# Delta-rule recurrence with a feed-forward: the first three chunks and the last taken unit by unit

## The chip, the cores and the metric

The kernel runs on one core of a Trainium2 chip. The metric is the device time of one execution in microseconds. The core has five engines with queues of their own: TensorE (PE; its weight loads are listed apart as PEld), VectorE (DVE), ScalarE (ACT), GpSimd (POOL) and SyncE (SP, which issues most DMAs).

## The reference

Two stages, one behind the other. The first is a gated delta rule over 768 time steps for 4 batches and 8 heads of width 48; the second is a feed-forward of width 2048 with a tanh GELU on the 3072 tokens of 384 values that come out of the first.

```python
k_n = k / (np.linalg.norm(k, axis=-1, keepdims=True) + 1e-06)
state = np.zeros((B, H, D, D))
for t in range(S):
    y[:, :, t] = np.einsum('bhd,bhde->bhe', q[:, :, t], state)
    v_old = np.einsum('bhde,bhd->bhe', state, kt)
    state = state + bt[..., None, None] * np.einsum('bhd,bhe->bhde', kt, vt - v_old)
x = y.transpose(0, 2, 1, 3).reshape(B * S, H * D)
h = x @ w_in
g = 0.5 * h * (1.0 + np.tanh(c * (h + 0.044715 * h * h * h)))
return g @ w_out
```

## The kernel before, in words

Time is cut into 12 chunks of C = 64 steps. The partition axis holds two batches of 64 steps each, so a chunk has two units of 128 rows, unit u = 2c + x with x = 0, 1; the units of one chunk belong to different batches and share no state.

`prep(u)` makes what a unit needs and what does not depend on the state: it normalises k (`kn`), multiplies by beta (`kb`), casts q (`qb`), transposes all three (`T` on PE and the copy `kT` for the first six units, a transposing DMA on SP behind them), takes two products of the transposed tiles (`G2` and `G`, L624 and L616), masks them into `ln` and `wp` (DVE), and inverts a triangular 64 x 64 matrix for each head by five rounds. A round is a product on PE (`A`, L665), a subtraction from 2I on DVE (`rt` or `rl`, L679), a second product (`B`, L665) and a copy out of PSUM into the block-diagonal tile `bd` or the result `xi` (L448 on ACT or DVE, L647 and L651 on POOL).

`chain(c)` is the recurrence over chunks, for both units at once: state times k (`K`, L720), minus v (`R`, L730, on DVE), state times q (`Q`, L720), inverse times that (`U`, L742), its copy `us` (`Un`), the new state (`S`, L751, and `Sn`), the output (`O`, L765), its copy `xo` (`On`), and the transposition of the output into `xT` (`X`, L787 and a copy, or a transposing DMA for chunks 4 to 10). `U`, `K`, `Q`, `S` and `O` are 32 matmuls each on small tiles of the PE array (64 x 64 or 48 x 64); the products of the inverse and the feed-forward use the full 128 x 128 array.

`mlp(gi)` is the feed-forward of one chunk, 256 tokens: 48 up matmuls (`up`, L809, 128 columns of W1 against 256 tokens, in groups of three), a GELU on ACT for every 4 of the 16 slices (`gelu`, L814, 128 x 1024), 2 x 16 down matmuls (`down`, L822, 384 columns, in groups of four), a copy `ob` (`Z`) and two output DMAs for each 128 tokens. W1 and W2 are loaded by POOL's DMA queue (L546, L550).

The order of the work on each engine is fixed when the program is built. Class `Flow` collects the steps with a duration, a key and the tiles read and written; `schedule()` is a planner that plays the engines forward in time and takes the ready step of the lowest key, with rules for PSUM banks, for PE's changes between full and small tiles (`SWITCH`, `PEN`, `GLUE`), for its clock and for blocks of 256 instructions (`BLOCK`, `REFILL`). `KEYS` shifts the key of every kind of step and `EXTRA` that of one kind in one part (`F.part`, the chunk) of the kernel. 110 matmuls on a tile of zeros (`fill`, L505) have the highest key and are placed where PE has nothing else ready; those left over stand at the end of PE's queue. `emit()` writes each engine's queue out with semaphore waits; an engine never leaves its queue's order at run time.

Of the kernel before, what the change touches and what calls it, by code (L numbers as in the profile page):

```python
# [14 lines left out]
C = 64  # L15
# [9 lines left out]
class Flow:  # L25
# [5 lines left out]
    SLACK = 0.128241  # L31
# [3 lines left out]
    STALL_SLACK = 0.120045  # L35
    YIELD = 0.372832
    KEYS = {"A": (-12.24992, -5.03297), "B": (-9.6185, -29.0564), "G": (-8.95358, -2.60127), "G2": (-14.50399, -54.31342),
# [3 lines left out]
            "Z": (-21.81342, -68.60243), "bdc": (7.59004, 13.93148), "bde": (-0.21638, -43.1126), "bdz": (1.14496, 67.13998),  # L41
            "down": (12.66804, 33.19835), "eps": (30.23541, -44.34922), "gelu": (6.25889, 47.5543), "inv": (-36.99569, -17.04963),
            "kT": (21.81306, -1.95089), "kb": (-10.85643, 26.05958), "kn": (46.26391, 23.16738), "ladj": (-19.15066, 56.95864),
            "ln": (21.15613, -25.11016), "loadk": (6.01406, -22.83934), "loadq": (13.08921, -8.18376), "loadv": (3.59665, -5.26042),
            "out": (5.42829, -58.1066), "pow": (4.89602, -34.99663), "qb": (7.55526, 19.94565), "rt": (-22.59389, 3.94263),
            "sq": (-11.42456, 52.70149), "sum": (35.6419, -19.11125), "tabG": (-30.0791, 50.43816), "tri": (19.11756, -10.52721),
            "turn": (-4.97863, -20.83721), "turnx": (-24.1172, -42.56893), "up": (4.18149, -12.91155), "w1": (-25.34548, 32.61637),
            "w2": (31.31702, 12.2471), "wp": (0.57459, -43.94026), "xT": (-28.12189, -41.44086), "xi": (5.37624, -27.34308)}
    EXTRA = {"1eps.1": 5.8983, "1inv.1": -0.10911, "1pow.1": -12.59508, "1sq.1": 17.11214, "1sum.1": -2.50147, "1wz.0": -1.64746,
# [324 lines left out]
def bass_deltanet__then__act_gelu_tanh_kernel(  # L374
# [15 lines left out]
    GROUPS = [[c] for c in range(NC)]  # L390
# [9 lines left out]
    with nc.allow_non_contiguous_dma("strided loads"), nc.allow_low_precision("bf16 pipeline"):  # L400
# [173 lines left out]
        def prep(u):  # L574
            x, c = u % 2, u // 2
            z = "" if c else "0"
# [118 lines left out]
        def chain(c):  # L695
            ss = [(2 * c + x) % NP for x in range(2)]
            z = "" if c else "0"
# [3 lines left out]
            so, sn, son, snn = st[c % 2], st[(c + 1) % 2], f"st{c % 2}", f"st{(c + 1) % 2}"  # L701
            rb, rbn, ub, ubn, xb, xbn = rs[c % 2], f"rs{c % 2}", us[c % 2], f"us{c % 2}", xo[c % 2], f"xo{c % 2}"
            vr, vrn = raw["v"][c % NR], [f"vraw{c % NR}{x}" for x in range(2)]
            key = 2 * c + 0.5
            each = [(x, g) for x in range(2) for g in range(4)]

            def flat(ap):
                return ap.rearrange("p y x g d -> p y (x g d)")

            def banks(ap):  # L710
                return ap.rearrange("p (y r) -> p y r", y=2)[:, :, 0:DM]

            def at(name, P, r, b, x, g):
                o = 512 * b + 4 * D * x + D * g
                return P(ps(name))[r, o:o + D]

            def ks(e, P, y, name):
                for x, g in each:
                    for p, a in quad:
                        ins = e.matmul(at(name, P, hf(a), p, x, g), kT[ss[x]][hf(p, D), y, g, hf(a)], so[hf(p, D), a, x, g, :],  # L720
                                       start=(x == 0 and g == 0), stop=(y == 0), skip_group_check=True)
                return ins
            if first:
                for x in range(2):
                    A("act", z + "R0", lambda e, P, x=x: e.activation(
                        rb[:, :, x, :, :], vr[:, H * x:H * x + H, :].rearrange("p (g y) d -> p y g d", y=2), ACT.Copy, scale=-1.0), 0.5,
                      reads=[vrn[x]], writes=[rbn + "ab"[x]], key=key)
            else:
                A("pe", z + "K", lambda e, P: ks(e, P, 0, "K"), 0.28, reads=n("kT") + [son], alloc=(ps("K"), 2), mode="t", key=key, mm=32)
                A("dve", z + "R", lambda e, P: e.tensor_tensor(  # L730
                    rb[:, :, :, :, :].rearrange("p y x g d -> p y (x g) d"), banks(P(ps("K"))).rearrange("p y (g d) -> p y g d", d=D),
                    vr[:, :, :].rearrange("p (g y) d -> p y g d", y=2), ALU.subtract), 0.98,
                  reads=vrn, frees=[ps("K")], writes=[rbn + "a", rbn + "b"], key=key)
                A("pe", z + "Q", lambda e, P: ks(e, P, 2, "O"), 0.28, reads=n("kT") + n("xi") + [son, rbn + "a", rbn + "b"], alloc=(ps("O"), 2), mode="t",
                  key=key + 0.1, mm=32)
# [113 lines left out]
        for u in range(NU):  # L849
# [7 lines left out]
            if u % 2:  # L857
                chain(u // 2)
# [33 lines left out]
```

## Time and profile before

| | |
|---|---|
| timed runs | 278.71, 283.88, 285.86 us; median 283.88 |
| profiled execution | 278.1 us, of which the span from first to last instruction is 276.1 |
| mean granted TensorE clock | 0.994 |
| busy PE, DVE, ACT, POOL | 264.4, 193.8, 173.4, 142.5 us |
| first up matmul (L809), last down matmul (L822) ends | 46.33, 271.40 us |

The page's costliest groups are given as line, engine, operation, out<-in and the number, then busy time and mean length of one in ns, then the idle time of the engine just before them and what ended it. The slices cut the span into 40 equal parts; a digit is the busy share in tenths. Matmuls are pipelined, so the length of one is longer than its share of PE's time; the distance between the starts of two neighbouring groups is what a group costs.

```profile
L809 PE MATMUL ps<-xT,W 128*128 128x256 bf16 x576 | 81.7, 273 | 0.1
L822 PE MATMUL ps<-W,gT 128*128 128x384 bf16 x384 | 74.4, 326 | 0.1
L448 ACT ACTIVATE bd<-ps 64x512 bf16<-64x512 f32 x92 | 53.3, 589 | 20.2 <-PE ps L665 18.8
L814 ACT ACTIVATE gT<-ps 128x1024 bf16<-128x1024 f32 x48 | 48.6, 1023 | 18.2 <-PE ps L809 18.1
L679 DVE TENSOR_TENSOR rt<-ps,two 128x512 bf16<-128x512 f32 x72 | 48.6, 685 | 15.4 <-PE ps L665 15.0
```

### The profile page before, as it was taken

Reading aid. Unit: us, or ns where it says so; the run is one execution under the profiler, and the core shown is the slowest. Engines: PE = TensorE matmul, PEld = TensorE weight load, DVE = VectorE, ACT = ScalarE, POOL = GpSimd, SP = SyncE. Lnnn points to the kernel's source line nnn. Section 1 sums busy time; section 2 is a strip of 40 time slices with the busy share of each in tenths; the row PEclk is TensorE's granted clock in tenths of the full one; section 3 lists DMA queues with packets and bytes.
Section 4 is the critical chain, followed back from the end, with each engine's and each line's share of the span. In section 5 each row is a group of like instructions: output and inputs, shape, how many; then the busy total and the mean of one; then the engine's idle time right before and its main releaser. Section 6 shows DMA issues by size and latency. Waiting matters only on the chain.

```text
span 276.1 us, 12595 instructions
## 1 busy us (share of the span) xinstructions
PE 264.4 (96%) x5684; PEld 199.6 (72%) x5696; DVE 193.8 (70%) x308; ACT 173.4 (63%) x265; POOL 142.5 (52%) x214
## 2 busy tenths in 40 slices
PE   8999767999999999899999999999999999999999
PEld 3656456877777766786785878788788767996864
DVE  8899985898559989787978789677784638551000
ACT  5845474786847769885674566677777434875530
POOL 3178162689927985997958876245242403220000
PEclk9999997999999999999999999999999999999999
DMA  7999999993996977897299943717520282300213
GB/s 122 168 149 193 188 191 161 151 169 74 195 167 146 179 133 151 156 158 108 58 139 127 168 96 70 135 33 139 96 59 2 62 145 51 43 2 2 57 31 85
DMA packets 116309, 31.49 MB, mean 114 GB/s; under 512 B 110368, under 2 KB 115488, under 8 KB 116256
## 3 DMA queue, kind: packets, MB, share of 16 engines
q1 hardware_dynamic: 111920, 27.24, 60.7%
q0 software_dynamic: 2880, 3.15, 7.0%
q8 instruction: 45, 0.74, 1.2%
q10 hardware_dynamic: 1456, 0.30, 0.6%
q14 instruction: 8, 0.07, 0.1%
HBM read 20.64 MB, written 4.72 MB: 92 GB/s over the span
## 4 chain that ended last, share of the span: by engine, by line
PE 88%; DVE 5%; issue 2%; ACT 2%; DMA 2%
PE ps L822 23%; PE ps L809 22%; PE ps L665 18%; PE ps L505 9%; PE ps L742 3%; PE ps L616 3%; PE ps L720 2%; DMA kT<-tok 2%; PE ps L765 2%; PE ps L624 2%; PE ps L600 2%; DVE rt L679 1%; PE ps L751 1%; DVE wp L633 1%; ACT bd L448 1%
## 5 line engine op out<-in xcount | busy, mean ns | idle before, releaser
L809 PE MATMUL ps<-xT,W 128*128 128x256 bf16 x576 | 81.7, 273 | 0.1
L822 PE MATMUL ps<-W,gT 128*128 128x384 bf16 x384 | 74.4, 326 | 0.1
L448 ACT ACTIVATE bd<-ps 64x512 bf16<-64x512 f32 x92 | 53.3, 589 | 20.2 <-PE ps L665 18.8
L814 ACT ACTIVATE gT<-ps 128x1024 bf16<-128x1024 f32 x48 | 48.6, 1023 | 18.2 <-PE ps L809 18.1
L679 DVE TENSOR_TENSOR rt<-ps,two 128x512 bf16<-128x512 f32 x72 | 48.6, 685 | 15.4 <-PE ps L665 15.0
L809 PEld LDWEIGHTS ps<-xT,W 128*128 128x128 bf16 x576 | 48.9, 98 | 6.0
L647 POOL TENSOR_SCALAR_AFFINE_SELECT bd<-ln 64x512 bf16<-64x512 bf16 x48 | 31.5, 656 | 37.3 <-DVE ln L628 32.7
L822 PEld LDWEIGHTS ps<-W,gT 128*128 128x128 bf16 x384 | 33.8, 98 | 17.4 <-ACT xi L448 0.2
L651 POOL COPY bd<-xi 64x256 f32<-64x256 f32 x64 | 25.4, 398 | 36.7 <-ACT xi L448 27.6
L448 ACT ACTIVATE xi<-ps 128x512 bf16<-128x512 f32 x48 | 28.3, 596 | 13.7 <-PE ps L665 13.2
L633 DVE CAST_PREDICATED wp<-mup,ps 128x1024 bf16<-128x1024 uint16 x24 | 29.0, 1214 | 1.2 <-PE ps L616 1.0
L505 PE MATMUL ps<-wz 128*128 128x512 bf16 x98 | 27.7, 411 | 2.1 <-DVE wz L454 1.3
L448 DVE CAST bd<-ps 64x512 bf16<-64x512 f32 x36 | 24.6, 688 | 6.5 <-PE ps L665 5.9
L665 PE MATMUL ps<-rt,bd 128*128 128x64 bf16 x576 | 28.6, 193 | 0.6 <-DVE rt L679 0.3
L679 DVE TENSOR_TENSOR rl<-ps,two 128x384 bf16<-128x384 f32 (+1 forms) x48 | 23.1, 487 | 8.4 <-PE ps L665 7.9
L665 PE MATMUL ps<-wp,bd 128*128 128x64 bf16 (+1 forms) x576 | 27.6, 188 | 1.4 <-DVE wp L633 0.4
L665 PEld LDWEIGHTS ps<-wp,bd 128*128 128x128 bf16 x576 | 23.2, 97 | 7.0 <-DVE wp L633 1.7
L568 POOL TENSOR_TENSOR nrm<-nrm,half 128x16 f32<-128x16 f32 x9 | 26.1, 2908 | 3.7 <-DVE nrm L565 3.4
L665 PEld LDWEIGHTS ps<-rt,bd 128*128 128x128 bf16 x576 | 23.5, 98 | 4.7 <-DVE rt L679 1.8
L592 POOL TENSOR_TENSOR tok<-tok,bsb 128x384 bf16<-128x384 bf16 x23 | 19.0, 843 | 14.9 <-PE ps L751 8.7
L448 ACT ACTIVATE ob<-ps 128x384 f32<-128x384 f32 x21 | 10.3, 491 | 18.3 <-PE ps L822 18.1
L628 DVE CAST_PREDICATED ln<-mlo,ps 128x512 bf16<-128x512 uint16 x24 | 16.5, 687 | 6.4 <-PE ps L624 6.1
(83 smaller groups left out, 329.3 us busy)
## 6 DMA issues: line engine op xcount, KB each, us to landing
qraw<-in_q_dram SPq DMA_DIRECT2D x24, 192.0 KB, 5.1
vraw<-in_v_dram SPq DMA_DIRECT2D x24, 192.0 KB, 5.0
out_dram<-ob SPq DMA_DIRECT2D x48, 96.0 KB, 2.4
kraw<-in_k_dram SPq DMA_DIRECT2D x22, 192.0 KB, 5.0
W<-in_moe_w_in_dram POOLq DMA_DIRECT2D x2, 768.0 KB, 10.2
W<-in_moe_w_out_dram POOLq DMA_DIRECT2D x2, 768.0 KB, 14.8
kT<-tok SPq DMA_TRANSPOSE x18, 5.1
kraw<-in_k_dram ACTq DMA_DIRECT2D x2, 96.0 KB, 3.1
```

The costliest lines, as they stand in the source:

```text
L448: return e.activation(out, in_, ACT.Copy) if e is nc.scalar else e.tensor_copy(out, in_)
L505: ins = e.matmul(P(name)[:, :], wz[:, 0:128], wz[:, 0:512])
L568: e.tensor_tensor(nr[:, 1, hx], nr[:, 0, hx], half[:, hx], ALU.pow), {"act": 0.22, "pool": 1.65 * wd},
L592: A(POOL, z + "kb", lambda e, P: e.tensor_tensor(kb, kn, bcol, ALU.mult), tt, reads=[n("tok0"), *BS], writes=[n("tok1")], key=u)
L633: A("dve", z + y, lambda e, P, lo=lo, hi=hi: e.copy_predicated(wp[s][:, :, lo:hi], mup[:, lo:hi].bitcast(U16).unsqueeze(1).to_broadcast([1 ...
L647: A("pool", z + "X1", lambda e, P, src=src, dst=dst: e.affine_select(out=dst, in_=src, compare_op=ALU.not_equal, fill=1.0, base=0, pattern ...
L651: A("pool", z + "bdc", lambda e, P, src=src, dst=dst: e.tensor_copy(dst.bitcast(F32), src.bitcast(F32)), 0.42, reads=[n("xi")], writes=[w( ...
L665: ins = e.matmul(P(name)[:, C * h + lo:C * h + C], bd[m][:, h, :], rhs[:, h, lo:C], start=not add, stop=True, skip_group_check=add)
L679: e, r_[:, :, lo:C], P(ps(f"A{i}")).rearrange("p (h t) -> p h t", h=H)[:, :, lo:C]) if u < ADD else e.tensor_tensor(
L809: ins = e.matmul(P(ph)[:, w * f:w * f + w].rearrange("p (x t) -> p x t", x=2), W1[:, j, 128 * (i + f):128 * (i + f) + 128], x_[:, :, j, :] ...
L814: A("act", z + "gelu", lambda e, P, i=i, ph=ph: e.activation(g_[:, i:i + nf, 0:w], P(ph).rearrange("p (f t) -> p f t", f=nf), ACT.Gelu_app ...
L822: ins = e.matmul(P(po)[:, 0:DM], g_[:, f, 128 * b:128 * b + 128], W2[:, f, :], start=(f == 0), stop=(f == FC - 1))
```

## The change

`chain` and `mlp` take a list `xs` of the units of the chunk that they work on. For the first three chunks (`HALVES`) and the last (`TAIL`) they are called for one unit at a time, as soon as that unit is prepared; the other eight chunks are called for both units, as before. A call for one unit issues 16 small-tile matmuls in place of 32 for each step of the recurrence, copies of half the width, three transposes in place of six, and 48 up matmuls of 128 columns for 128 tokens, with a GELU of 128 x 1024 for every 8 slices. The tiles `st`, `rs`, `us`, `xo`, `xT` and `gT` are tracked by unit and not by chunk. The number of GELUs, down matmuls, loads and outputs stays. `F.part` is the unit in place of the chunk, so `EXTRA` has an entry by kind and unit, and all the planner's constants, `KEYS` and `EXTRA` have new values; so the order of the work on every engine is another throughout.

```diff
-    SLACK = 0.128241
+    SLACK = 1.796034
...
-    STALL_SLACK = 0.120045
-    YIELD = 0.372832
...
+    STALL_SLACK = 7.031178
+    YIELD = 0.145092
...
-    PEN = 3.376955
-    HOLD = 0.200936
-    SOON = 0.200469
-    GLUE = 4.720138
-    PATIENCE = 0.264186
-    HASTE = 0.586658
+    PEN = 3.089705
+    HOLD = 0.543568
+    SOON = 0.261360
+    GLUE = 3.285667
+    PATIENCE = 0.831901
+    HASTE = 8.000000
...
-    PHASE = 1.896137
+    PHASE = 0.429894
...
-    GROUPS = [[c] for c in range(NC)]
+    HALVES, TAIL = 3, 1
...
-        def chain(c):
+        def chain(c, xs):
             ss = [(2 * c + x) % NP for x in range(2)]
-            z = "" if c else "0"
-            n = lambda y: [f"{y}{s}" for s in ss]
-            ps = lambda y: f"{y}.{c}"
+            x0, nx = xs[0], len(xs)
+            sl = slice(x0, x0 + nx)
+            z = "" if 2 * c + x0 else "0"
+            n = lambda y: [f"{y}{ss[x]}" for x in xs]
+            m = lambda y, i: [f"{y}{i}{x}" for x in xs]
+            ps = lambda y: f"{y}.{c}.{x0}"
...
-            key = 2 * c + 0.5
-            each = [(x, g) for x in range(2) for g in range(4)]
+            key = 2 * c + (0.5 if nx == 2 else x0)
+            tt = 0.16 + 0.00107 * 384 * nx
+            each = [(x, g) for x in xs for g in range(4)]
...
-            A("pe", z + "U", umat, 0.36, reads=n("xi") + [rbn + "a", rbn + "b"], alloc=(ps("U"), 2), mode="t", key=key, mm=32)
...
+            A("pe", z + "U", umat, 0.18 * nx, reads=n("xi") + rbn, alloc=(ps("U"), nx), mode="t", key=key, mm=16 * nx)
...
-        def mlp(gi):
-            g = GROUPS[gi]
+        def mlp(c, xs):
             z = ""
-            w = 256 * len(g)
...
+            x0, nx = xs[0], len(xs)
+            sl, w = slice(x0, x0 + nx), 128 * nx
+            ts = slice(128 * x0, 128 * x0 + w)
...
             nf = 1024 // w
...
         for u in range(NU):
-            F.part = u // 2
+            F.part = u
...
             prep(u)
-            if u % 2:
-                chain(u // 2)
-            for gi, g in enumerate(GROUPS):
-                if u == 2 * g[-1] + 1:
-                    mlp(gi)
+            c = u // 2
+            for xs in ((u % 2,),) if c < HALVES or c >= NC - TAIL else ((0, 1),) if u % 2 else ():
+                chain(c, xs)
+                mlp(c, xs)
```

More of the change, by code (lines that the diff above doesn't have):

```diff
@@ L575, in prep @@
             x, c = u % 2, u // 2
-            z = "" if c else "0"
+            z = "" if u else "0"
             r, s = c % NR, u % NP
@@ L765, in omat @@
                             ins = e.matmul(at("O", P, hf(a), p, x, g), wp[ss[x]][hf(a), 4 * p + g, C:2 * C], ub[hf(a), x, p, g, :],
-                                           start=first and x == 0 and g == 0, stop=True, skip_group_check=True)
+                                           start=first and x == x0 and g == 0, stop=True, skip_group_check=True)
                 return ins
-            A("pe", z + "O", omat, 0.36, reads=[ubn] + n("wq"), mode="t", key=key + 0.2, mm=32, fence=True,
+            A("pe", z + "O", omat, 0.18 * nx, reads=ubn + n("wq"), mode="t", key=key + 0.2, mm=16 * nx, fence=True,
@@ L769, in chain @@
               **(dict(alloc=(ps("O"), 2)) if first else dict(accum=[ps("O")])))
[L770 to L776 removed]
+            A(EV, z + "On", lambda e, P: copy(e, xb[:, sl, :].rearrange("p x (g y d) -> p y x g d", y=2, g=4),
+                                    banks(P(ps("O"))).rearrange("p y (x g d) -> p y x g d", x=nx, g=4)), ev(384 * nx),
+              frees=[ps("O")], writes=xbn, key=key + 0.2)
@@ L781, in chain @@
                 return
             def trans(e, P):
-                for x in range(2):
+                for x in xs:
                     for j in range(J):
-                        o = DM * x + 128 * j
+                        o = DM * (x - x0) + 128 * j
                         ins = e.transpose(P(ps("X")).bitcast(BF16)[:, o:o + 128], xb[:, x, 128 * j:128 * j + 128], ident[:, :])
                 return ins
-            A("pe", z + "X", trans, 0.35, reads=[xbn, "ident"], alloc=(ps("X"), 1), mode="m", key=key + 0.3, mm=6)
@@ L802, in mlp @@
             nf = 1024 // w
             for i in range(0, FC, nf):
-                ph = f"H.{gi}.{i}"
+                ph = f"H.{c}.{x0}.{i}"
                 for f in range(nf):
@@ L814, in mlp @@
-                A("act", z + "gelu", lambda e, P, i=i, ph=ph: e.activation(g_[:, i:i + nf, 0:w], P(ph).rearrange("p (f t) -> p f t", f=nf), ACT.Gelu_apprx_tanh),
-                  1.03, reads=["one"], frees=[ph], writes=[f"{gn}.{i + f}" for f in range(nf)], key=key + 0.5 * span * i / FC)
-            for b in range(w // 128):
-                po = f"Z.{gi}.{b}"
-                kz = key + 0.5 * span * (1 + b * 128 / w)
+                    A("pe", z + "up", up, J * (0.000422 * w if nx == 2 else 0.056), reads=xn + [f"W1{0 if i < FC // 2 else 1}"], mode="m", key=key + 0.5 * span * i / FC, mm=J,
+                      **(dict(alloc=(ph, 2), writes=m(f"{gn}s{i}")) if f == 0 else dict(accum=[ph])))
@@ L819, in mlp, with down @@
+                A("act", z + "gelu", lambda e, P, i=i, ph=ph: e.activation(g_[:, i:i + nf, ts], P(ph).rearrange("p (f t) -> p f t", f=nf), ACT.Gelu_apprx_tanh),
+                  1.03, reads=["one"], frees=[ph], writes=sum([m(f"{gn}.{i + f}") for f in range(nf)], []), key=key + 0.5 * span * i / FC)
+            for x in xs:
+                po = f"Z.{c}.{x}"
+                kz = key + 0.5 * span * (1 + (x - x0) / nx)
                 for i in range(0, FC, 4):
-                    def down(e, P, i=i, b=b, po=po):
+                    def down(e, P, i=i, x=x, po=po):
@@ L821, in down @@
                         for f in range(i, i + 4):
-                            ins = e.matmul(P(po)[:, 0:DM], g_[:, f, 128 * b:128 * b + 128], W2[:, f, :], start=(f == 0), stop=(f == FC - 1))
+                            ins = e.matmul(P(po)[:, 0:DM], g_[:, f, 128 * x:128 * x + 128], W2[:, f, :], start=(f == 0), stop=(f == FC - 1))
                         return ins
-                    A("pe", z + "down", down, 4 * 0.163, reads=[f"{gn}.{f}" for f in range(i, i + 4)] + [f"{gn}s{i}", f"W2{0 if i < FC // 2 else 1}"],
+                    A("pe", z + "down", down, 4 * 0.163, reads=[f"{gn}.{f}.{x}" for f in range(i, i + 4)] + m(f"{gn}s{nf * (i // nf)}") + [f"W2{0 if i < FC // 2 else 1}"],
@@ L842, in bass_deltanet__then__act_gelu_tanh_kernel @@
         for c in range(3):
-            F.part = c
+            F.part = 2 * c
             norms(c)
```

97 lines of the change are left out of this document (46 added, 51 removed), and 124 rows, old and new, of tables (EXTRA, KEYS).

## The prediction, made before the changed kernel had run

> **What bounds the kernel now.** I read the page first: the engine shares, the slices, then the costliest groups.
>
> ```profile
> PE 264.4 (96%) x5684; PEld 199.6 (72%) x5696; DVE 193.8 (70%) x308; ACT 173.4 (63%) x265; POOL 142.5 (52%) x214
> ...
> PE   8999767999999999899999999999999999999999
> ...
> DVE  8899985898559989787978789677784638551000
> ...
> L505 PE MATMUL ps<-wz 128*128 128x512 bf16 x98 | 27.7, 411 | 2.1 <-DVE wz L454 1.3
> ```
>
> PE looks full from end to end, but L505 is the zero matmul that fills PE's waits. Of the 110 in PE's queue, 75 stand ahead of the first feed-forward matmul, 14 behind it, 21 at the very end. So there are two regimes: to about 46 us PE waits for DVE (9s in slices 3 to 5, of 6.9 us each), after that PE itself is the bound. The chain of waits shows the hand-over (columns: start, length, what):
>
> ```profile
> 40.58 0.27 PE ps L720 x19
> 40.85 2.63 issue
> 43.48 0.28 PE ps L720 x13
> ...
> 46.52 0.64 PE ps L809 x3
> ```
>
> The reader is to see a pause inside one group of 32 like matmuls, with nothing waited for. The timeline has 126 matmuls, with their loads 252 PE instructions, between an earlier pause of 0.58 us in L742 (ended 36.47) and the end of this one (43.48): instructions arrived late, a block of them in 7.0 us. A table by stretch shows what followed: a clock of 0.57.
>
> ```profile
> 44.00:48.00 4.00, 4.00 (x79) 3.43 (x75) 3.23 (x5) 2.47 (x5) 1.47 (x1) 0.57 1.10 164
> ```
>
> The timeline gives PE's prices, read from start to start, and the end:
>
> ```profile
> 180.53 0.81 PE L822 MATMUL ps<-W,gT 128*128 128x384 bf16 x4
> 181.18 0.40 PE L665 MATMUL ps<-wp,bd 128*128 128x64 bf16 x8
> 181.51 0.42 PE L616 MATMUL ps<-kT 48*64 48x128 bf16 x16
> ...
> 55.32 0.83 PE L600 MATMUL ps<-ident,tok 128*128 128x128 bf16 x12
> 55.99 0.40 PE L665 MATMUL ps<-rt,bd 128*128 128x64 bf16 x8
> ...
> 271.40 4.48 PE L505 MATMUL ps<-wz 128*128 128x512 bf16 x20
> ```
>
> Four down matmuls: 0.65 us. Eight of the inverse: 0.233 elsewhere, but 0.33 here, since the next group is of small tiles: a change between full and small tiles costs 0.10 us, and as much on the way back (L616 to L822: 0.35 against 0.25 from L616 to L720 at 182.84). Twelve transposes of 128 columns, each with its own load: 0.67, 56 ns each. Twelve up matmuls of 256 columns: 1.31 (209.73 to 211.04), 109 ns each. The last down matmul ends at 271.40, and filling runs on to 275.88.
>
> **The sum by PE's queue.** A sum of these prices over the queue of before, from the first up matmul (46.33) to the last filler, gives 224.7 us; it took 229.55. So 4.85 us there are waits and late instructions. The changed program's queue is known from its build, so the same sum can be made for it, part by part.
>
> *Up matmuls.* Four chunks (0, 1, 2, 11) go in halves: 192 matmuls of 256 columns become 384 of 128. By the row: 384 x 55.8 ns = 21.4 against 192 x 109.2 = 20.9: +0.5 us. The Trainium skill speaks against this: "TensorE: Matmul & The Clock Gate", section "Back-to-back issue gap", gives about 81 ns for each load and matmul pair of 128 columns in a real kernel. By it this term would be +10 us. The trace does not agree so far (56 ns; 29 ns with 64 columns), but has no up matmul of 128 columns, so it stays a rival.
>
> *Small-tile groups.* The recurrence of chunks 0, 1, 2 and 11 runs as 16 matmuls per unit in place of 32 (in chunks 3 to 10 nothing changes). The matmuls are as many, but the queue changes tile size 198 times, not 154; behind the first up matmul 188 against 140: +4.8 us. This is the largest cost, and nothing hides it, as PE is the bound there.
>
> *Copies on DVE and ACT.* Halved copies pay their fixed part twice: the page has 0.49 us for 384 columns on ACT against 0.81 for 768. DVE's queue sums to 205.6 us of rows against 195.2. Both engines have room behind 46 us (DVE 70%), so I take nothing; without that cover it would be at most the 10 us, spread over 230.
>
> *DMA, SP, POOL.* As many loads, outputs and transposes. Four outputs of early units stand ahead of loads in SP's queue; a late load would show behind 60 us, where rows have POOL waiting at most 5.6 us for one, off PE's path: nothing. W's second part has one cast, one product and two memsets more ahead of it on POOL (0.5 + 0.84 + 2 x 0.48 by their rows): issued by 26.8 at worst in place of 24.5 and landed within 17.0, 43.8. The first down matmul stands 9.3 us of rows behind the first up matmul, so at some 45: nothing, but with little cover, and a later landing would be paid in full.
>
> *Fillers.* 72 ahead of the first up matmul, 15 behind it, 23 at the end: behind it 38 x 0.216 against 35: +0.65.
>
> *Moved work.* The first up matmul now needs one unit, so 5.4 us of rows (mostly inverse, transposes) move behind it.
>
> Sum from the first up matmul: 224.7 + 0.5 + 4.8 + 0.65 + 5.4 = 236.0 by the queue's sum. It must therefore start 11.3 us sooner, at 35.0, to break even.
>
> **When it starts.** DVE carries the start. Up to the first output copy (row 60 of DVE's queue) its rows sum to 38.0 us and it ended at 39.4, so 1.4 idle. The changed queue reaches the copy into xT of unit 0 after 28.1 us of rows: not before 29.5. From above: unit 0's first inverse product at 16.4 (one wp copy and one transpose group sooner than 17.75), five rounds at the shared pace of before (17.75 to L742 at 35.39: 17.6), and 4 for the steps to the up matmul: 38.0. Unit 0 is now served ahead of unit 1; stepping through its chain by single rows (product 0.4, rt 0.6, product 0.4, bd 0.65, with DVE's other rows in between) I get 32.5, and take 33.3 with a little for waits: 1.7 sooner than needed.
>
> **Late instructions.** Before pays its two pauses and the cold clock ahead of 46.33. The changed queue uses up its third to fifth block of 256 instructions in 4.1, 4.7 and 5.9 us of rows, at about 33 to 46 us, while W and the inputs still load. At an arrival every 6.4 us (before's block that ended at 36.47 had begun near 30.08) this costs 2.3 + 1.7 + 0.5 = 4.5; at 7.0 it is 2.9 + 2.3 + 1.1 = 6.3; nothing if PE's other waits there stretch the use of the blocks that far. I take 2.5: the waits of the start cover most of the first block's share, not the second's. "Runtime: NRT & Kernel Launch" in the Trainium skill, section "Instruction fetch mechanics", calls such a crossing mostly hidden. By it the term is nothing; the 2.63 us pause above says otherwise.
>
> So 33.3 + 236.0 + 4.85 + 2.5 = 276.7 against 275.9: +0.8 us, a profiled execution of 278.9 against 278.1. That one was the fastest of four: the timed runs were 278.71, 283.88 and 285.86. All four average 281.6, 3.5 above the profiled one. I add this: **282.4 us**, 0.5% under the median of 283.88. About 2% is what a measurement of this kernel can tell from no change.
>
> **Rivals.** *The start pays more* (35%). Finer steps give PE something else to do where it waited, so the pauses go and the residue falls: start 32.5, residue 2.0, no late block: 32.5 + 236.0 + 2.0 = 270.5, 5.4 less, so 276.2 timed (-2.7%). For it: the two pauses and the clock of 0.57 come from the dense groups of 32, now 16. Against it: behind 46 us only 4.85 was to be had.
>
> *Instructions come too late* (19%). At 7.0 us a block the three blocks cost 6.3, and two pauses over 2 us bring the clock down as at 44 to 48 us, 1.8 each: 33.3 + 236.0 + 4.85 + 6.3 + 3.6 = 284.1, 8.2 more: 289.8 timed (+2.1%). It decides from about 6.9 us a block. For it: 384 more PE instructions, earlier, under a DMA share of 1.1 to 1.3. Against it: small tiles are spread out.
>
> *128 columns cost 81 ns* (6%). 384 loads and matmuls at a pitch of 81 ns, a load-bound pitch that no row shows: 9.7 more than the forecast, 292.1 (+2.9%).
>
> *The start is not brought forward* (4%): if DVE alternates between the units as before, 38.0 in place of 33.3: 4.7 more, 287.1 (+1.1%), no change.
>
> The forecast has 36%. Faster by over 2%: the first rival with two points of the forecast's lower edge, 37%. Slower: 19 + 6 = 25%. Within: 38%. The range from 273 to 290 reaches from the first rival, with runs nearer the profiled one, to the second.
>
> **What would show it.** Right: the first up matmul at 32 to 35; 128-column groups of three at 0.17 us start to start; 0.10 us at each change of tile size; the last down matmul near 271, fillers to 276. Wrong: pauses of "issue" over 2 us before 50 us, a PE clock under 0.9 there, PE waiting for xT or W, or "issue" and DVE waits of PE behind 60 us over 5 us in sum.

## The result, and the profile after

The changed kernel takes 290.19 us (median of 4 runs, 288.78 to 290.40), with 281.85 us (278.71 to 285.86) for the kernel before beside it: ratio 1.038, interval 1.0314 to 1.0447, slower. Here and below the ratio leaves out runs of a kernel that took over 1.5% longer than its fastest at a lower granted clock, so it can differ from the ratio of the medians. The profiled execution took 290.06 us, its span is 288.3 us, 12.2 more than before, and the mean granted clock is 0.976.

The page, with the shares of the engines, PE's slices and the clock in tenths:

```profile
PE 274.6 (95%) x5888; PEld 205.9 (71%) x5888; DVE 204.7 (71%) x330; ACT 168.8 (59%) x260; POOL 143.7 (50%) x216
...
PE   8999389999999999997989999999999999999999
...
PEclk9999787999999999998999999999999999999999
...
PE 78%; SPq 5%; DMA 5%; DVE 4%; POOL 3%; ACT 3%; issue 2%; POOLq 0%
```

PE has a hole in slice 5 (28.8 to 36.0 us) that was not there before, and the clock falls in slices 5 to 7 and again near 135 us. The shares of the chain of waits at the end show three entries that the forecast set at nothing: SP's queue and a DMA with 5% each, POOL with 3%. The chain of waits, taken up to 48 us, names them:

```profile
15.88 14.11 DMA qraw<-in_q_dram
29.99 0.05 issue
30.04 0.50 POOL tok L524
30.55 0.21 POOL W L626
...
34.38 0.58 PE ps L741 x8
```

A load of q (unit 4, the first of chunk 2) took 14.11 us to land. The timeline of POOL, first before and then after, shows what stood behind it (start, length, what; in brackets the idle time before it and its releaser):

```profile
17.73 1.75 POOL L546 DMA_DIRECT2D W<-in_moe_w_in_dram  x2
...
25.41 0.97 POOL L448 CAST tok<-qraw 128x384 bf16<-128x384 f32 x2
```

```profile
16.14 1.75 POOL L622 DMA_DIRECT2D W<-in_moe_w_in_dram  x2
...
30.04 0.50 POOL L524 CAST tok<-qraw 128x384 bf16<-128x384 f32 x1 [6.44 <-DMA qraw<-in_q_dram]
30.49 1.82 POOL L626 DMA_DIRECT2D W<-in_moe_w_out_dram  x2
32.30 0.52 POOL L524 CAST tok<-qraw 128x384 bf16<-128x384 f32 x1
32.76 1.47 POOL L723 TENSOR_SCALAR_AFFINE_SELECT bd<-ln 64x512 bf16<-64x512 bf16 x2
```

After, the cast of that q stands at the head of POOL's queue for 6.44 us. Behind it, in the fixed order, stand the issue of W2 and two selects that build a block-diagonal tile for unit 3. The timeline of PE shows who wanted them:

```profile
28.85 0.60 PE L581 MATMUL ps<-wz 128*128 128x512 bf16 x2
34.38 0.58 PE L741 MATMUL ps<-wp,bd 128*128 128x64 bf16 x8 [4.93 <-POOL bd L723]
34.89 0.62 PE L822 MATMUL ps<-rs,xi 64*64 64x48 bf16 x16
...
38.76 0.38 PE L889 MATMUL ps<-xT,W 128*128 128x128 bf16 x3
```

Unit 3's inverse product (L741) waited 4.93 us, and behind it in PE's queue stood unit 0's `U` (L822), on which everything up to the first up matmul (L889) hangs. So a load for chunk 2 held up the recurrence of chunk 0, by way of two queues. Then the clock: the table by stretch (length, then busy time and number for PE, PEld, DVE, ACT, POOL, then the clock) has 0.50 where the first chain runs.

```profile
34.40:38.00 3.60, 3.60 (x77) 3.04 (x78) 1.25 (x2) 1.16 (x3) 0.00 (x0) 0.50 1.28 190
```

Later, two more things are to be seen. In the timeline, one group of 16 `G` products is cut by a pause in which nothing is waited for, and the eight down matmuls behind it go at half the clock (2.75 us; elsewhere 1.47):

```profile
132.37 0.25 PE L692 MATMUL ps<-kT 48*64 48x128 bf16 x3
133.98 0.41 PE L692 MATMUL ps<-kT 48*64 48x128 bf16 x13 [1.35 <-issue]
...
134.67 2.75 PE L902 MATMUL ps<-W,gT 128*128 128x384 bf16 x8
...
282.94 5.13 PE L581 MATMUL ps<-wz 128*128 128x512 bf16 x23
```

The whole of PE's queue can be summed up in each trace from start to start of its matmuls, in four parts: rows (each matmul at its price), changes of tile size (0.10 us each), what the halved clock added, and the rest, which is waits of every kind. The third column is an experiment from below that takes POOL's wait away.

| us | before | changed | changed, W1 issued later |
|---|---|---|---|
| rows | 241.5 | 241.9 | 241.9 |
| changes of tile size | 15.2 | 19.6 | 19.6 |
| halved clock | 1.9 | 6.2 | 1.9 |
| waits | 15.6 | 18.7 | 16.0 |
| first up matmul at | 46.33 | 38.76 | 33.88 |
| span | 276.1 | 288.3 | 281.3 |

(The kernel before lacks 12 filling matmuls in its records, 2.6 us; they are put under rows and taken from waits. The four parts leave out 1.9 us of each span, most of it ahead of the first matmul. A stretch of 3.41 us at half the clock can cost at most 1.7, so the split between the last two parts is rough, by some 0.2 us for each stretch; their sum does not depend on it.) The 12.2 us are 0.4 of rows, 4.4 of changes, 4.3 of halved clock and 3.1 of waits.

### The profile page after: what moved, and what is told of

Its sections match the earlier page's. It is cut to its first block, busy times and chain, and to the rows that moved or that the text cites. A ratio compares the mean times of both kernels' runs of the same rounds, so it can differ in the third digit from the quotient of the medians.

```text
span 288.3 us, 12993 instructions
## 1 busy us (share of the span) xinstructions
PE 274.6 (95%) x5888; PEld 205.9 (71%) x5888; DVE 204.7 (71%) x330; ACT 168.8 (59%) x260; POOL 143.7 (50%) x216
## 4 chain that ended last, share of the span: by engine, by line
PE 78%; SPq 5%; DMA 5%; DVE 4%; POOL 3%; ACT 3%; issue 2%; POOLq 0%
PE ps L889 22%; PE ps L902 22%; PE ps L741 18%; DMA qraw<-in_q_dram 5%; SPq L613 5%; PE ps L846 3%; PE ps L800 3%; PE ps L581 2%; PE ps L822 2%; PE ps L692 2%; PE ps L700 1%; PE ps L832 1%; ACT bd L524 1%; DVE bd L524 1%; POOL bd L723 1%
## 5 line engine op out<-in xcount | busy, mean ns | idle before, releaser
L889 PE MATMUL ps<-xT,W 128*128 128x128 bf16 (+1 forms) x768 | 85.7, 247 | 1.2 <-issue 1.0
L902 PE MATMUL ps<-W,gT 128*128 128x384 bf16 x384 | 76.9, 331 | 0.3 <-DVE xi L524 0.3
L524 ACT ACTIVATE bd<-ps 64x512 bf16<-64x512 f32 x84 | 49.3, 590 | 30.1 <-PE ps L741 29.1
L889 PEld LDWEIGHTS ps<-xT,W 128*128 128x128 bf16 x768 | 55.4, 98 | 7.8 <-issue 1.1
L894 ACT ACTIVATE gT<-ps 128x1024 bf16<-128x1024 f32 x48 | 48.5, 1022 | 19.8 <-PE ps L889 19.6
L755 DVE TENSOR_TENSOR rt<-ps,two 128x512 bf16<-128x512 f32 x72 | 48.8, 685 | 15.6 <-PE ps L741 15.0
L902 PEld LDWEIGHTS ps<-W,gT 128*128 128x128 bf16 x384 | 33.3, 99 | 17.2 <-issue 1.0
L524 DVE CAST bd<-ps 64x512 bf16<-64x512 f32 x44 | 30.1, 688 | 8.0 <-PE ps L741 7.2
L524 ACT ACTIVATE xi<-ps 128x512 bf16<-128x512 f32 x37 | 21.9, 596 | 21.8 <-PE ps L741 21.4
L741 PE MATMUL ps<-wp,bd 128*128 128x64 bf16 (+1 forms) x576 | 27.9, 190 | 6.0 <-POOL bd L723 5.1
L581 PE MATMUL ps<-wz 128*128 128x512 bf16 x110 | 30.8, 405 | 1.5 <-DVE wz L530 1.3
L741 PEld LDWEIGHTS ps<-wp,bd 128*128 128x128 bf16 x576 | 23.2, 99 | 11.1 <-issue 5.7
L741 PE MATMUL ps<-rt,bd 128*128 128x64 bf16 x576 | 29.2, 195 | 0.4 <-DVE rt L755 0.2
L741 PEld LDWEIGHTS ps<-rt,bd 128*128 128x128 bf16 x576 | 24.2, 99 | 5.0 <-DVE rt L755 2.1
L668 POOL TENSOR_TENSOR tok<-tok,bsb 128x384 bf16<-128x384 bf16 x24 | 19.9, 839 | 14.3 <-PE ps L832 7.9
L666 POOL TENSOR_TENSOR tok<-kraw,nrm 128x384 bf16<-128x384 f32 x22 | 17.9, 829 | 9.5 <-DVE nrm L648 9.3
L524 ACT ACTIVATE ob<-ps 128x384 f32<-128x384 f32 x23 | 11.3, 491 | 15.6 <-PE ps L902 15.5
```

Source lines behind the costliest of these rows:

```text
L524: return e.activation(out, in_, ACT.Copy) if e is nc.scalar else e.tensor_copy(out, in_)
L581: ins = e.matmul(P(name)[:, :], wz[:, 0:128], wz[:, 0:512])
L668: A(POOL, z + "kb", lambda e, P: e.tensor_tensor(kb, kn, bcol, ALU.mult), tt, reads=[n("tok0"), *BS], writes=[n("tok1")], key=u)
L741: ins = e.matmul(P(name)[:, C * h + lo:C * h + C], bd[m][:, h, :], rhs[:, h, lo:C], start=not add, stop=True, skip_group_check=add)
L755: e, r_[:, :, lo:C], P(ps(f"A{i}")).rearrange("p (h t) -> p h t", h=H)[:, :, lo:C]) if u < ADD else e.tensor_tensor(
L889: ins = e.matmul(P(ph)[:, w * f:w * f + w].rearrange("p (x t) -> p x t", x=nx), W1[:, j, 128 * (i + f):128 * (i + f) + 128], x_[:, sl, j, ...
```

## The experiments

Times beside a run are those of the kernel before on the same chip. The runs were made on four chips: those on POOL's wait, in both kernels; then the changes of tile size, the first of the two runs with long matmuls and the end of the kernel before; then the second of them, all three edits together and the first three chunks alone; last VectorE. Between these groups the traces are compared, and times only roughly. In most experiments a helper reorders an engine's finished queue between `schedule()` and `emit()`: `_reorder(F, engine, [(first, last, to)])` moves the entries first to last ahead of the entry `to`. A second one, `_shift`, moves entry i of one engine's queue to place j of another's. They shift the line numbers by 36, or by 44 with the second.

### POOL's wait: two ways to take it out of the changed kernel

The selects first: unit 3's two selects (entries 33, 34) go ahead of the cast that waits for q (29).

```diff
         F.schedule()
+        _reorder(F, "pool", [(33, 34, 29)])
         F.emit(nc, psum)
```

> The changed kernel with one move in POOL's queue: the two selects that make unit 3's first block-diagonal tile stand ahead of the cast of unit 4's q, which waited 6.44 us for its load; all else in the same order. Theory (the head of POOL's queue holds up PE): PE's pause of 4.93 us behind 29 us is gone, the first up matmul starts at 33 to 35 in place of 38.8, the two stretches of clock 0.5 and 0.6 between 34 and 50 us go or shrink, and the time falls from 290.2 to 281 to 285. Rival (the wait only moves on: to W's second part, which is still issued behind the cast, at some 30 us, or to late instructions): the first up matmul comes sooner, but pauses of as many microseconds appear before 55 us, and the time stays at 288 or more.

284.46 us (282.88 to 286.64) beside 279.15: ratio 1.022 (1.009 to 1.035). POOL's timeline, and then PE's at the first up matmul:

```profile
27.08 1.45 POOL L759 TENSOR_SCALAR_AFFINE_SELECT bd<-ln 64x512 bf16<-64x512 bf16 x2 [3.27 <-DVE ln L740]
30.19 0.50 POOL L560 CAST tok<-qraw 128x384 bf16<-128x384 f32 x1 [1.66 <-DMA qraw<-in_q_dram]
```

```profile
33.12 0.34 PE L925 MATMUL ps<-xT,W 128*128 128x128 bf16 x3
```

The load of q is as late as before (30.19), and it no longer matters: the selects are done at 28.5 and the first up matmul stands at 33.12. So it was the order on POOL's queue that turned a late load into a late first up matmul.

W1 later: the issue of W1 (entries 19, 20) goes behind two casts and two products (ahead of 25).

```diff
         F.schedule()
+        _reorder(F, "pool", [(19, 20, 25)])
         F.emit(nc, psum)
```

> The changed kernel with one move in POOL's queue: the issue of W's first part stands behind two casts and two products of the second chunk, at about 19 us in place of 16.1; all else in the same order. Theory (W's first part, issued 1.6 us sooner than before, got into the DMA rings ahead of the third chunk's q, which took 14.1 us to land in place of 5): the q lands by 25, POOL does not wait for it, PE's pause of 4.93 us is gone, and the time is 281 to 285. Rival (the load is late because four v loads follow it or because of the general crowd): it still takes over 10 us to land, the pause stays over 3 us, and the time is within 2 us of 290.

284.13 us (282.82 to 286.74), ratio 1.019 (1.008 to 1.031); first up matmul at 33.88. POOL's timeline, and in a second view the landing of the q loads:

```profile
19.63 1.75 POOL L658 DMA_DIRECT2D W<-in_moe_w_in_dram  x2
...
24.51 0.50 POOL L560 CAST tok<-qraw 128x384 bf16<-128x384 f32 x1
```

```profile
DMA to landing us min/median/max: 3.5/4.7/6.2
```

The same row in the changed kernel, and then in the kernel before:

```profile
DMA to landing us min/median/max: 3.7/4.9/14.1
```

```profile
DMA to landing us min/median/max: 3.5/5.1/6.1
```

With W1 issued at 19.63 in place of 16.14 the cast does not wait at all. Both edits together:

```diff
+        _reorder(F, "pool", [(33, 34, 29), (19, 20, 25)])
```

> The changed kernel with both moves of the two runs before. Theory: as each alone, 281 to 285, since either takes the same wait away; if W's second part, issued sooner too, was a hidden second cost, 1 to 2 us less than the better of the two. Rival (the two do different things): the sum of two partial gains, clearly below both.

286.07 us (284.71 to 286.20), ratio 1.024 (1.016 to 1.032). The start is that of the run before (33.86), but the halved clock costs 5.5 us here (39.1 to 45.9 and 131.3 to 134.7) where it cost 1.9 there. The two edits do not add up. The runs of the three kernels overlap (282.88 to 286.64, 282.82 to 286.74, 284.71 to 286.20), so none of them is shown to be the fastest.

### The same wait, made in the kernel before

The issue of W1 goes ahead of the second pair of selects of unit 1, from 17.73 to 16.03 us.

```diff
         F.schedule()
+        _reorder(F, "pool", [(18, 19, 16)])
         F.emit(nc, psum)
```

> The kernel before with the mirror move: the issue of W's first part stands ahead of the second pair of selects in POOL's queue, at some 16.2 us in place of 17.7, as in the changed kernel. Theory: the third chunk's q lands late here too (over 10 us from issue, 5 in the kernel before), POOL's cast waits for it with the selects of the second chunk behind it, PE pauses for some 4 us before 35 us, and the time rises by 4 to 8 us. Rival (1.5 us do not decide; the changed kernel's load order does): the q lands in 5 to 8 us and the time stays within 2 us of the kernel before.

283.10 us (281.03 to 283.79): ratio 1.013 (1.004 to 1.022). POOL's timeline, and the landing of the q loads:

```profile
16.03 1.75 POOL L582 DMA_DIRECT2D W<-in_moe_w_in_dram  x2
...
30.34 1.81 POOL L586 DMA_DIRECT2D W<-in_moe_w_out_dram  x2 [6.88 <-DMA qraw<-in_q_dram]
```

```profile
DMA to landing us min/median/max: 4.0/5.2/14.1
```

1.7 us sooner for W1's issue is enough to make one q load land after 14.1 us in place of at most 6.1, and POOL wait 6.88 us. The first up matmul moves from 46.33 to 49.48. This happens without any of the change, so it goes with when W1 is issued, not with units alone.

The packets in the traces show how. The loads of q and v go in packets of 192 bytes, some 850 in each microsecond, until W1's packets of 2 KB begin (at 18.23 us in the changed kernel). From 19 to 27 us, while W1 moves at 65 to 101 packets a microsecond, the loads from SP get 0 to 96; in the two microseconds behind it they get 694 and 950, and the q load lands at 29.99. In the kernel before W1's packets begin at 19.63, and the same q load lands at 20.85. The slow stretch meets two v loads there, which take 15.3 and 19.7 us to land; their first use on DVE stands at 43.8, and nothing waits for them.

### What a change of tile size costs

40 small products are added to the kernel before, each inside an up product of full tiles and so between two full-tile matmuls; their result is overwritten.

```diff
                         for j in range(J):
+                            if j == 2 and f == 0 and gi > 1:
+                                e.matmul(P(ph)[0:64, 512:560], wz[0:64, 0:64], wz[0:64, 0:48])
```

> The kernel before, with 40 small products more: in the first up product of each hidden tile of chunks 2 to 11, between the second and the third matmul, one 64x64-tile matmul of 48 zero columns is written into the still unused second bank of the same hidden tile. Both neighbours are full-tile matmuls of the same product, so each adds exactly two changes of tile size and one row of about 12 ns; the output stays what it was. If a change of tile size costs TensorE the 0.09 to 0.10 us that the gaps of the changed kernel show, each of the 40 costs 0.2 + 0.012 us: +8.5 us, about 287.6 beside 279.15. Rival, changes hidden behind waits that TensorE has anyway: its waits behind the first up product are 5.3 us in the kernel before, so at least 3 us stay, and the time is 279 to 283. If the price were a matter of the longer records only (no change at all), +0.5.

The control has the same 40 products on the full tile:

```diff
+                                e.matmul(P(ph)[:, 512:560], wz[:, 0:128], wz[:, 0:48])
```

> The control: the same 40 products at the same places, 48 zero columns, but on the full 128x128 tile, so no change of tile size. The price of one is near the 29 ns of an inverse product of 64 columns: 40 x 0.025 = +1.0 us, about 280.2 beside 279.15. If it is as slow as the run with changes of tile size, the price is one of the added instructions and not of the changes.

288.44 us (287.74 to 289.13) with changes, ratio 1.038 (1.034 to 1.043); 284.47 us (279.21 to 286.51) with full tiles, ratio 1.007 (1.002 to 1.011); beside them 278.72. The two ratios differ by 3.2% of 278.7, 8.8 us, for 80 changes. The timelines show the same at one place (small tile, then full tile):

```profile
179.20 0.71 PE L811 MATMUL ps<-xT,W 128*128 128x256 bf16 x5
179.84 0.21 PE L810 MATMUL ps<-wz 64*64 64x48 bf16 x1
179.98 0.50 PE L811 MATMUL ps<-xT,W 128*128 128x256 bf16 x3
```

```profile
180.74 0.71 PE L811 MATMUL ps<-xT,W 128*128 128x256 bf16 x5
181.28 0.19 PE L810 MATMUL ps<-wz 128*128 128x48 bf16 x1
181.31 0.60 PE L811 MATMUL ps<-xT,W 128*128 128x256 bf16 x4
```

Five up matmuls and the added one take 0.78 us from start to start with the change (179.20 to 179.98), 0.57 without (180.74 to 181.31). Over the 40 places the medians are 202 + 139 ns against 109 + 28: 204 ns for two changes, 0.10 each, and nothing hides them.

### The pause inside the group at 132 us

Six long matmuls on zeros (1.30 us, 12 instructions) were to stand ahead of the dense stretch of small matmuls before the pause. The first try put them at the wrong place: units 6 and 7 belong to chunk 3, and the edit named chunk 7, so they ran at 213 to 217 us.

```diff
                         for j in range(J):
+                            for _ in range(3 if j == 2 and c == 7 and i == 12 and f < 2 else 0):
+                                e.matmul(P(ph)[:, 512:1024], wz[:, 0:128], wz[:, 0:512])
```

> The changed kernel, with six long matmuls (512 zero columns, 0.216 us each, 1.30 us in all, 12 instructions) added inside the up products of chunk 7 just ahead of the dense stretch U, G, inverse, G2, G (96 small matmuls in about 3 us) in which TensorE stood 1.35 us for instructions at 132.6 and behind which the clock was halved for 3.4 us (1.8 us of work lost). Late instructions: the long matmuls give the supply 1.30 us for 12 instructions (7.0 us per 252: 0.33 us), 0.97 us of lead, so the pause shrinks from 1.35 to about 0.4, and with it the halved window goes: net 1.30 - 0.97 - 1.8 = -1.5 us, or +0.3 if the window stays. Rival, the pause is a wait for data or goes with the queue's place, not with the supply: the six cost what they take, +1.3 us.

290.29 us (289.36 to 291.81): the pause at 133.7 us is still there (1.08 us), as it must be. With `c == 3` in place of `c == 7`:

> The run before this one had its six long matmuls at 213 us, in chunk 7, and not ahead of the pause, which lies behind the up products of chunk 3 (units 6 and 7). Here they are in chunk 3: six matmuls of 512 zero columns (1.30 us, 12 instructions) in the first two up products of its last hidden tile, at about 130 us, ahead of the dense stretch U, G, inverse, G2, G. Late instructions: the supply gets 1.30 us for 0.33 us of instructions (12 of 252 in 7.0 us), so the pause of 1.35 us shrinks to about 0.4 us; with the halved clock behind it gone (1.8 us) the time is that of the changed kernel less 1.5, about 288.7, and +0.3 if a halved stretch stays. Rival, the pause is a wait for data or belongs to the place in the queue: pause as long as before, +1.3 us, about 291.5.

289.19 us (288.63 to 290.79); the profiled execution took 288.63 us, 1.4 less than the changed kernel's, with 1.30 us more work. The runs of the two overlap, so by the times a gain is not shown. PE's timeline:

```profile
130.50 0.81 PE L890 MATMUL ps<-wz 128*128 128x512 bf16 x3
...
133.83 0.32 PE L700 MATMUL ps<-kT 48*64 48x64 bf16 x16
134.29 0.42 PE L692 MATMUL ps<-kT 48*64 48x128 bf16 x16
134.67 0.41 PE L741 MATMUL ps<-wp,bd 128*128 128x64 bf16 x8
134.91 1.46 PE L904 MATMUL ps<-W,gT 128*128 128x384 bf16 x8
```

The 16 `G` products now run through (0.42 us), and the down matmuls behind them go at the full clock (1.46). Work that needs few instructions, put in ahead, took the pause away. By itself that does not tell a wait for instructions from one for data, since 1.30 us more work ahead shortens either. The DMA queue that brings instructions tells them apart. In the page of the changed kernel it has 46 packets of 16 KB (packets, MB, share of 16 engines):

```profile
q8 instruction: 46, 0.75, 1.2%
```

The pause that ended at 133.98 did so 1.48 us behind the end of one of these packets, and the one that ended at 149.95 did so 1.52 behind another. Over all traces of this study, 56 of the 58 pauses of PE over 0.25 us that are put down to "issue" ended 1.3 to 1.8 us behind such a packet, while the packets come some 6 us apart. So these pauses are waits for instructions.

### The end of the queue

The kernel before without the filling matmuls behind the last down product:

```diff
         F.schedule()
+        while F.queues["pe"][-1].name == "fill":
+            F.ops.remove(F.queues["pe"].pop())
         F.emit(nc, psum)
```

> The kernel before, without the 21 filling matmuls that stand behind the last down product at the end of TensorE's queue. In its profile SyncE's last wait is 1.2 us for TensorE. If these fillers set the end, the span falls by 1.2 us, from 279 to about 278, and the time by as much; rival, the last output's DMA ends as late (its landing is within the same microsecond): no change. The difference is near the spread of the runs, so the spans and the last waits decide.

277.42 us (276.93 to 284.36) beside 278.72: ratio 0.997 (0.994 to 1.001). The span is 275.6. Its median is the lowest of this study, but the interval reaches 1, so a gain is not shown.

The changed kernel with W1 later, the six long matmuls and no filling at the end:

> The changed kernel with three edits together: W1's issue behind the casts (as in the run that issued it later: 284.1), the six long matmuls of chunk 3, and no filling matmuls behind the last down product. If the three causes are apart, it is 284.1, less 0.7 (0.97 us of pause gone is the most, for 1.30 us of matmuls; so between -0.7 and +0.4), less 1.3 (the end fillers took 1.3 us off the kernel before): 282 to 283.2, still behind the kernel before, since 4.4 us of changes of tile size (44 x 0.10) and the halved clock of 34 to 50 us stay. Rival, the kernel before is reached (279 or less): then the changes of tile size are not on the path that ends last.

284.39 us (283.37 to 285.08), so a miss: no better than W1 later alone (284.13, on another chip). The end behaves as expected (4.2 us from the start of the last down matmul to the end of the span, in place of 5.6), but at 143.1 us another pause for instructions of 1.37 us stands where there was one of 0.64, with a halved clock from 145.2 to 148.6 behind it. So what was taken away at 132 us was lost again there.

### The first three chunks alone

```diff
-    HALVES, TAIL = 3, 1
+    HALVES, TAIL = 3, 0
```

> One part of the change alone: the first three chunks go unit by unit, the last chunk's feed-forward goes for both units at once as before. The order of the first 60 us is that of the changed kernel. If what was lost is all in the start and in the late instructions, the time is that of the changed kernel within 1 us (289 to 291), with the same wait of POOL for q (about 6.4 us) and the first up product at 38 to 39 us. If the last chunk's part is a gain of its own (its down products start earlier, nothing is left over at the end), it is slower than the changed kernel by up to 2 us; if it is a loss of its own, faster by as much, 288.

289.05 us (286.99 to 291.85). POOL waits 6.30 us for q and the first up matmul stands at 38.60, as in the changed kernel. From there to the last down matmul it takes 242.2 us in place of 244.2; the halved clock costs 1.05 us less (no halved stretch at 134) and the waits 0.6 less. That leaves 0.3 for the last chunk's part, which by this count brings and costs next to nothing; most of the loss is in the first three chunks.

### VectorE behind the first up matmul

With W1 issued later, 4.8 us of halved clock (1.9) and waits (2.9) were left from 33.9 to 50 us. The table by stretch of that run has DVE full there, not PE:

```profile
34.00:38.00 4.00, 2.59 (x59) 1.93 (x58) 3.94 (x8) 3.03 (x6) 0.89 (x2) 1.00 1.27 185
38.00:42.00 4.00, 3.55 (x85) 2.62 (x84) 3.88 (x7) 1.72 (x4) 3.10 (x5) 0.78 1.27 185
```

So two copies of 0.69 us were moved from DVE to ACT, and in a second run two from ACT to DVE, both on top of W1 later.

```diff
+        _shift(F, [("dve", 64, "act", 46), ("dve", 62, "act", 45)])
```

> The changed kernel with W1's issue behind the casts (284.1, first up product at 33.9), and two copies bd of the inverse (64x512, 0.69 us each, for units 1 and 3, which VectorE did at 39.5 and 40.9) done by ScalarE instead, behind the copy of the same kind that it does there; ScalarE stood idle from 40.6 to 42.8. VectorE stays the bound behind the first up product: from 33.5 to 44.0 us its rows stand without a gap, while TensorE has 10.1 us of rows in the 16.1 us from 33.9 to 50. Taking 1.4 us off VectorE there makes the waits and the halved clock of TensorE in that stretch (4.8 us in sum) 0.7 to 1.4 us shorter; 282.7 to 283.4, and 1.4 to 2.7 under the run with two copies more on VectorE. Rival, TensorE's own instructions and clock bound that stretch: no change, waits and halved clock 4.8 us in sum, and no difference between the two runs.

```diff
+        _shift(F, [("act", 45, "dve", 64), ("act", 44, "dve", 62)])
```

> The opposite of the run before: the two copies bd that ScalarE did at 39.0 and 40.0 (units 1 and 3) are done by VectorE ahead of its own, 1.4 us of rows more on VectorE. If VectorE is the bound from 34 to 44 us, TensorE's waits and halved clock from the first up product to 50 us grow from 4.8 to 5.5 to 6.2 us, and the time from 284.1 to 284.8 to 285.5. Rival as before: no change.

284.26 us (283.07 to 286.03) with less on DVE, 287.47 (286.52 to 288.02) with more. More costs: halved clock and waits up to 50 us grow from 4.8 to 6.6 us, and another halved stretch follows at 115.6. Less brings nothing: 5.0 us. PE's timeline with less on DVE shows why.

```profile
38.00 0.22 PE L844 MATMUL ps<-st,kT 48*64 48x48 bf16 x4 [0.81 <-issue]
...
43.58 0.20 PE L785 MATMUL ps<-rl,bd 128*128 128x64 bf16 x1
44.86 0.36 PE L785 MATMUL ps<-rl,bd 128*128 128x64 bf16 x7 [1.08 <-issue]
```

PE gets to the second group sooner, and then stands in the middle of it for 1.08 us (0.35 with W1 later alone). It goes on at 44.86, there at 44.68: 127 matmuls and 6.86 us behind the end of the pause at 38.00, near the 7.0 us for 126 in the kernel before and the 6.7 for 126 with W1 later alone. So in this stretch, as the two runs suggest, two limits lie side by side, DVE's rows and the arrival of instructions; taking off the one uncovers the other.

## Why the prediction was wrong

**Where the 11.4 us are.** The forecast's sum put PE's end at 276.7; it came at 288.1. Of the difference 5.5 is the first up matmul (38.76 for 33.3), 5.9 lies behind it.

**The step that failed first: "DMA, SP, POOL", which the forecast set at nothing.** It asked how much more work stands ahead of W2's issue on POOL, found 26.8 us at worst, and checked W2's landing against the first down matmul. It did not ask what the entry at the head of POOL's queue itself waits for. W2 was issued at 30.49, behind a cast that stood 6.44 us for a load, and what counted behind it was not W2 but two selects, and behind them, on PE, another unit's `U`. W1's issue came 1.6 us sooner than before, which the forecast did not see as a cost: the run in the kernel before shows that this alone makes the q load late. The forecast looked for a late load behind 60 us; it stopped POOL from 23.6 to 30.0.

**When it starts** was right as a term of its own: with the selects first, or W1 later, the first up matmul stands at 33.1 and 33.9, beside 33.3.

**Rows and changes of tile size** were right: 236.0 forecast, 235.8 by the new trace's own prices from the first up matmul on, fillers included. The 0.10 us for each change, which the forecast called the largest cost that nothing hides, was borne out by its own experiment. The up matmuls of 128 columns go at 56 ns, as the transposes of before did. PE's timeline of the changed kernel, 18 of them in 1.01 us:

```profile
55.13 1.17 PE L889 MATMUL ps<-xT,W 128*128 128x128 bf16 x18
56.14 0.40 PE L741 MATMUL ps<-rt,bd 128*128 128x64 bf16 x8
```

So the rival that went with the Trainium skill ("TensorE: Matmul & The Clock Gate", section "Back-to-back issue gap", about 81 ns) falls.

**Late instructions** had the right size by chance, at the wrong place: 2.5 forecast for 33 to 46 us, 2.8 found as two pauses at 132 (1.58) and 149 us (1.19), read start to start. At 33 to 46 us POOL's wait had let the instructions come up; with that wait gone they cost 1.0 at 37 us and 0.4 at 44. What the Trainium skill says in "Runtime: NRT & Kernel Launch", section "Instruction fetch mechanics", that a crossing is mostly hidden, agrees by number (46 packets and two such pauses in the changed kernel), but not for the places where small matmuls stand close: the two cost 2.8 us.

**The residue of 4.85 us** was carried over from before, and this is the second step that failed. With the late instructions the forecast had 7.35 behind the first up matmul; about 13.2 came: 3.7 of halved clock, 2.8 of late instructions and 6.7 of other waits. The forecast held that PE is the bound from the first up matmul on. That was read where it stood before, at 46 us. Moved to 34, it stands where DVE's rows are still without gaps, and "both engines have room behind 46 us" covers nothing there. DVE is not the only limit there: with 1.4 us taken off it, the late instructions showed in its place. The halved clock follows the waits and was in the forecast for a rival only.

**What the whole start was worth.** By the table, with POOL's wait gone waits and halved clock are 17.9 us, in the kernel before 17.5. The forecast expected about 13.7 (6.3 ahead of 33.3, by the queue's sum, and 7.35 behind it). The first up matmul comes 12.5 us sooner, and yet PE waits as long in all; the waits have only moved behind it. What is left is the price of the new order: 4.4 of tile changes, 0.4 of rows and 0.4 of waits, in sum the 5.2 us by which that run's span is longer.

**The 3.5 us added at the end**, for the distance of the timed runs of before from its profiled one, hid a third of the miss by luck: the changed kernel's runs lie at its profiled time. Against the profiled 278.9 the miss is 11.2 us, against the 282.4 on record 7.8.

**The rivals.** "Instructions come too late" gave 289.8, close to what was measured, but not by that way: its pauses behind 33 us cost 2.8 and not 6.3. What delayed the start was POOL, which no rival named. Two things stay open. Why the clock is halved in one run and not in another with like pauses is not settled. And the planner's constants were changed together with the units, so no run shows how much of the 44 more changes of tile size, and of the order on POOL, comes from the units and how much from the constants.

## What to carry to other kernels

When the order is fixed at build time, read at every moved entry what the entry ahead of it waits for, on each queue up to the one that counts: one late load at the head of a helper's queue can stop another unit's work two queues on. Bringing the first step of the next stage forward gains nothing by itself; sum up the waits of the bounding engine, and ask whether they shrink or only move. Splitting groups of small tiles has a price for each change of tile size (0.10 us here), and where that engine is the bound it is paid in full. Before a large load is moved forward, ask which small-packet loads are still under way then: it slows them.

## What the runs showed of the hardware

An issue of a weight load 1.6 to 1.7 us sooner made a q load, issued at about the same time on another queue, land after 14.1 us in place of at most 6.1, in both kernels; with W1 issued 3.5 us later no q load took more than 6.2. While 2 KB packets of W1 moved, at 65 to 101 a microsecond, the queue of 192-byte packets fell from some 850 a microsecond to at most 96.

The pauses for instructions stand at fixed counts of matmuls, whatever the time. Counted in the traces of the changed kernel and of its versions without long matmuls, most come behind 474, 601, 1870, 2250, 2630 and 3011 matmuls (give or take one): steps of 127 or its multiples (380 is three times 126.7). Single ones stand behind 1361 and 1615, which fit the same steps. In the kernel before the counts are 468, 594, 1733 and 2236.

The clock was halved in stretches of 3.4 us or two or three times that. Of the 25 in the traces that began while PE had work, 17 began during a wait of about 1 us or more or within 2.2 us of its end (134.4 behind the pause that ended at 133.98, 40.2 behind that of 38.01 with W1 later), but not every such wait had one. Changing between full and small tiles cost 0.09 to 0.10 us each way.
